# Reordering small products and first attention scores in a fused RWKV, tanh feed-forward and top-1 expert kernel

## The chip, the cores and the metric

The kernel runs on one core of a Trainium2 chip. The core has five engines that work side by side, each through its own instructions in a fixed order: TensorE (PE in the profile, with PEld for loading weights), VectorE (DVE), ScalarE (ACT), GpSimd (POOL) and SyncE (SP), which here issues transfers. The metric is the device time of one execution in microseconds (us); less is better.

## The reference

Three stages follow each other, in fp32:

```python
# 1. RWKV attention: B=4, H=8, S=768, D=48; state (D x D) for each batch and head
for t in range(S):
    cur = einsum(u * k_t, v_t)                    # outer product
    y[t] = r_t @ (state + cur)
    state = w[:, None] * state + outer(k_t, v_t)
x = y as (3072, 384)
# 2. feed-forward, w_in (384, 2048), w_out (2048, 384)
h = x @ w_in
x = (h - tanh(h)) @ w_out
# 3. top-1 mixture of 8 experts, w1 (8, 384, 1024), w2 (8, 1024, 384)
logits = normed(x) @ normed(expert_emb).T / tau   # argmax picks the expert, softmax its weight
out[mask_e] = gate[mask_e] * (relu(x[mask_e] @ w1[e]) @ w2[e])
```

## The kernel before, in words

**Tiles and blocks.** The 3072 tokens are 24 tiles of 128; tile n belongs to batch n % 4 and is that batch's chunk n // 4. Three tiles make a block of 384 columns, of which there are eight. The state of a batch is carried from chunk to chunk in `st`. Tiles 0 to 2 are block 0, tiles 3 to 5 block 1, tiles 6 to 8 the third block (j = 2).

**Attention of one tile.** The recurrence is written as products. Keys and queries are multiplied with tables of decays (`decay_k` on POOL or VectorE, `decay_r` on VectorE). `scores` (16 products into two PSUM banks `pa`) gives the scores of eight heads. `diagonal` writes a tile `am` for each half of the heads that holds the bonus term on its diagonal: eight small ScalarE copies for tiles 0 to 5, two POOL products from tile 6 on. `causal` (VectorE) copies the scores above it into `am`. `values` multiplies `am` and the old state into a bank `py`, `result` writes its high and low parts into the block's tile `xt`, `state` adds the tile's product to the state. For tiles 0 to 5 the keys are turned by TensorE into a bank (`turned`, `ps_k`) and copied out by ScalarE (`turned_rows`, `ktok`). From tile 6 on POOL makes `ktok` (`decayed`) and the bonus `rk` (`bonus`), which VectorE sums (`sums`). The five operations from the decay to `decayed` are a tile's head.

**Feed-forward.** Hidden block f (128 of 2048 columns) of a token block is nine products in `ffn1` (fp32 is split into a high and a low part, three products for each of three slices) into a bank `ph`; ScalarE and VectorE turn it into `ghi` and `glo`; `ffn2` adds nine products into three accumulator banks, three steps later (`LAG`, `PLAG`).

**Early steps.** The first 22 steps are hidden blocks 0 to 5 of block 0 and all 16 of block 1. Beside them the kernel converts the weights, which come as 64-bit floats in 16 pieces, into fp32 (three integer operations on VectorE, a copy `wq` on ScalarE, a subtraction on POOL, L267), and makes eight extra columns of w_out by which the expert logits fall out of `ffn2`. Such a `Logits` takes three steps: `turn` (six transpositions into two banks `pt`, two ScalarE copies into `wt`, a tag of two buffers), in the next step `product` (12 products into `pl`), in the one after it `back`. The turns are in steps 1, 2, 4, 7, 9, 12, 16 and 19. The attention of tiles 3, 4 and 5 begins in steps 1, 2 and 3 (`attention_stage`). Some steps have products of ones ahead of their hidden block (`fill`, `IDLE`), which compute nothing that is used.

**The last steps of block 0.** The loop over j follows: j = 0 does block 0's hidden blocks 6 to 15 (n = 0 to 9), then come blocks 2 to 7. The attention of block j + 1 runs beside block j as a generator of 18 pieces, six for a tile: head; scores and causal; two empty; values, state and result; empty. During j = 0 it is that of the third block; (n + 1) * 18 // 8 pieces have been drawn after step n. So tile 6's head and scores are drawn at n = 0, its values at n = 2, tile 7's head and scores at n = 3, its values at n = 4, tile 8's head at n = 5, its scores at n = 6 and its values at n = 7. Block 1's last accumulation is at n = 2, behind the pieces of that n. Its `finish` then copies three rows into tiles `xr` and stores them, finds the expert of each token, and computes the gates (with a POOL power and a ScalarE exponential, L673 and L678).

**What sets the order.** Up to `startup.close()` the order on each engine is that of the program. Behind it a planner orders each engine: among the instructions that its own simulated time makes ready it takes the one that stands first in the program. The buffers of a tag, PSUM banks included (eight, one tag), are given out again when the last user of the old tile is done. `rk` and `xr` share a tag of two buffers. `tc.issue_after(x)` puts the instructions in its block behind x on x's engine. `fence[6]` puts tile 6's head behind instructions of step 9.

Of the kernel before, what the change touches and what calls it, by code (L numbers as in the profile page):

```python
# [9 lines left out]
F32R = mybir.dt.float32r  # L10
# [3 lines left out]
AF = mybir.ActivationFunctionType  # L14
# [15 lines left out]
def rwkv__then__tanh_ffn__then__top1_moe_kernel(  # L30
# [14 lines left out]
    nc = tc.nc  # L45
# [6 lines left out]
    P = 128  # L52
    HP = H // 2
    NCH = S // P
    NK = DM // P
    TB = 3
    NB = NT // (TB * P)
    TOK = TB * P
# [16 lines left out]
    DACT = True  # L75
# [3 lines left out]
    NATT = 12  # L79
    NATT0 = 8  # L80
    ICOL = 6
# [130 lines left out]
    mark = {}  # L212
# [116 lines left out]
    class Att:  # L329
# [56 lines left out]

        def diagonal(self, on_act=False):
            self.am = []
            for g in range(2):
                a = work.tile([P, HP, P], F32, name="am", bufs=4)  # L390
                if on_act:
                    for q in range(HP):
                        nc.scalar.activation(out=a[:, q, :], in_=ident, func=AF.Copy, scale=self.cd[:, q, g:g + 1])
                else:
                    nc.gpsimd.tensor_tensor(out=a, in0=ident[:, None, :].to_broadcast([P, HP, P]),  # L395
                                            in1=self.cd[:, :, g:g + 1].to_broadcast([P, HP, P]), op=ALU.mult)
                self.am.append(a)
# [80 lines left out]

    def attn_tile(n, xt):
        t = Att(n, xt)  # L480
        with ExitStack() as es:
            for x in fence.pop(n, ()):
                es.enter_context(tc.issue_after(x))
            t.decay_r(nc.vector)
            t.decay_k(nc.gpsimd)
            t.bonus(nc.gpsimd)
            t.sums()
            t.diagonal()
            t.decayed()
        yield  # L490
        t.scores(range(HP))
        t.causal()
        yield
        yield
        yield

        t.values()
        t.state()
        t.result()
        yield  # L500
        yield

    xts = {}
    fence = {}
# [9 lines left out]
    def attention(j):  # L514
        xts[j] = work.tile([P, NK, 2, TOK], F32R, name="xt")
        for n in range(TB * j, TB * j + TB):
            if 2 * TB + 1 < n + 1 < NTILE:
                load_rkv(n + 1)
            yield from attn_tile(n, xts[j])

# [715 lines left out]
    def attention_stage(i):  # L1236

        later = []
        for n, first in zip(range(TB, 2 * TB), START):
# [6 lines left out]
            if i == first + 1:  # L1246
# [3 lines left out]
                t.turned()  # L1250
                t.diagonal(DACT)
                t.turned_rows()
            elif i == first + 2:
# [22 lines left out]
    def step2(j, i, g):  # L1276
        if i == spans[j][0]:
            accs[j] = [ps.tile([P, DL], F32, tag="p", name=f"acc{t}") for t in range(TB)]
        ffn2(i, spans[j], g, wout, accs[j])

    steps = [(0, f) for f in range(FA)] + [(1, f) for f in range(NF)]
    spans[0] = (0, FA)
# [3 lines left out]
    for i in range(len(steps) + 1):  # L1286
# [33 lines left out]
        for f in later:  # L1320
            f()
        if i in turns:
            c = turns[i]
            logits.append(Logits(c, ready[2 * c + 1][0]))
            logits[c].turn()
            done.add(2 * c + 1)
        if i - 2 in turns:
            logits[turns[i - 2]].back()
        if i - 1 in turns:
            logits[turns[i - 1]].product()  # L1330
        if m < NF:
# [3 lines left out]
        if i == 9:  # L1335
            fence[2 * TB] = mark["glo"], last[1]
        load_next()
# [4 lines left out]
        if i == ISTORE:  # L1342
            store_x(1, xts[1])
    del xts[1]

# [16 lines left out]
    for j in (0, *range(2, NB)):  # L1362
        xt = xts.pop(j)
        store_x(j, xt)
        att = attention(max(j + 1, 2)) if j + 1 < NB else iter(())
        na = 0
        natt = NATT if j > 0 else NATT0
        for n, i in enumerate(range(*spans[j])):
            ph = ffn1([win(p, i) for p in range(2)], columns_of(xt), NK, TOK)
            pend.append((j, i, small_tanh(ph, squares(ph), j * NF + i)))  # L1370
            while na < (n + 1) * 18 // natt:
                next(att, None)
                na += 1
# [103 lines left out]
```

## Time and profile before

| | |
|---|---|
| median of 3 runs | 812.74 us (811.16 to 815.42) |
| profiled execution | 813.03 us, of which the span from the first to the last instruction is 811.4 |
| mean granted TensorE clock | 0.980 of full speed |
| TensorE busy | 778.0 us (96% of the span) |
| VectorE, ScalarE, POOL busy | 506.7, 452.0 and 284.1 us |

Times in the profile count from the start of the span. A group of instructions is named by engine, source line and by the tiles that it writes and reads (`out<-in`). An entry in brackets gives the idle time of the engine just before the instruction and the instruction that ended it. The granted clock (PEclk) is 1.00 where TensorE had its 2.4 GHz for the whole stretch and 0.50 where it had 1.2 GHz. Ends of matmuls are modelled.

### The profile page before, as it was taken

The page shows a single profiled execution, that of the slowest core. Times are in us where ns is not written, and L with a number is a line of the kernel's source. Part 1 is how long each engine was busy: PE and PEld are TensorE (multiplying, and loading weights), DVE is VectorE, ACT ScalarE, POOL GpSimd, SP SyncE. Part 2 cuts the span into 40 slices and gives each one's busy share as a digit, 9 for nine tenths or more (in the row PEclk, how much of TensorE's full clock was granted, in tenths as well). Part 3 has the DMA queues.
Part 4 walks back from the last instruction along what each step waited for, and adds up shares of the span by engine and source line. Part 5 has one row for each costly group of instructions (what it writes and reads, how often), then busy time and mean ns, then how long its engine had stood idle before and what let it go on. Part 6 is the DMA issues. An engine that isn't in the chain of part 4 may idle for free. (4 is left out here: it accounts for less than half of the span.)

```text
span 811.4 us, 15572 instructions
## 1 busy us (share of the span) xinstructions
PE 778.0 (96%) x5938; PEld 729.3 (90%) x5938; DVE 506.7 (62%) x1080; ACT 452.0 (56%) x1044; POOL 284.1 (35%) x296
## 2 busy tenths in 40 slices
PE   8899999999999999999999999999899999999992
PEld 5679898889999999999999999999789999999992
DVE  7977974766765866875865865686544435554510
ACT  5676686547456556566566567684443444454421
POOL 3721640563550750750741610333340313331111
PEclk9899999999999999999999999999999999999997
DMA  8834350223330240331231210331733445554300
GB/s 275 284 89 134 111 194 1 85 83 122 106 114 23 67 155 21 83 125 43 86 116 54 86 45 15 120 96 31 229 102 118 137 129 166 175 171 143 111 28 30
DMA packets 41861, 87.33 MB, mean 108 GB/s; under 512 B 9744, under 2 KB 21440, under 8 KB 40754
## 3 DMA queue, kind: packets, MB, share of 16 engines
q1 hardware_dynamic: 37042, 76.74, 29.1%
q0 software_dynamic: 4320, 9.51, 3.6%
q8 instruction: 48, 0.79, 0.4%
q14 instruction: 35, 0.29, 0.2%
q10 hardware_dynamic: 416, 0.00, 0.0%
HBM read 67.46 MB, written 19.47 MB: 107 GB/s over the span
## 5 line engine op out<-in xcount | busy, mean ns | idle before, releaser
L534 PE MATMUL ph<-xt,wq 128*128 128x384 f32 (+2 forms) x1712 | 343.4, 343 | 2.2 <-ACT wt L284 1.4
L534 PEld LDWEIGHTS ph<-xt,wq 128*128 128x128 f32 x1712 | 304.2, 190 | 7.8 <-issue 1.7
L545 PE MATMUL acc<-wq,ghi 128*128 128x392 f32 (+2 forms) x1120 | 289.9, 344 | 0.9 <-ACT ghi L610 0.5
L545 PEld LDWEIGHTS acc<-wq,ghi 128*128 128x128 f32 (+1 forms) x1120 | 200.8, 187 | 6.5 <-issue 1.2
L545 PE MATMUL acc<-wq,glo 128*128 128x392 f32 (+2 forms) x560 | 185.6, 342 | 0.0
L581 ACT ACTIVATE z<-ph 128x384 f32<-128x384 f32 x128 | 62.6, 489 | 89.1 <-PE ph L534 88.6
L545 PEld LDWEIGHTS acc<-wq,glo 128*128 128x128 f32 (+1 forms) x560 | 104.3, 187 | 1.3 <-DVE glo L597 0.3
L592 ACT ACTIVATE ghi<-ph 128x384 fp32r<-128x384 f32 x128 | 62.7, 490 | 67.7 <-DVE ph L591 62.9
L590 DVE TENSOR_TENSOR ph<-ph,z 128x384 f32<-128x384 f32 x128 | 71.8, 561 | 45.2 <-ACT z L581 44.8
L597 DVE TENSOR_TENSOR glo<-ph,ghi 128x384 fp32r<-128x384 f32 x128 | 70.9, 554 | 40.9 <-ACT ghi L592 39.7
L764 POOL DMA_INDIRECT out_dram<-ob,gts x27 | 28.7, 1063 | 156.2 <-ACT ob L842 150.7
L582 ACT ACTIVATE q<-z,sb_t 128x384 f32<-128x384 f32 x128 | 78.9, 617 | 3.7
L591 DVE SCALAR_TENSOR_TENSOR ph<-q,ph 128x384 f32<-128x384 f32 x128 | 71.7, 560 | 12.0 <-ACT q L582 3.3
L611 DVE SCALAR_TENSOR_TENSOR glo<-ph,ghi 128x384 fp32r<-128x384 f32 (+2 forms) x56 | 31.4, 563 | 75.5 <-ACT ghi L610 59.8
L594 ACT ACTIVATE mk<-z,lz_t 128x384 bf16<-128x384 f32 x128 | 77.1, 602 | 0.0
L610 ACT ACTIVATE ghi<-ph 128x384 fp32r<-128x384 f32 (+2 forms) x56 | 27.7, 496 | 73.6 <-PE ph L534 72.5
L811 DVE TENSOR_TENSOR wq<-eraw,wq 128x768 fp32r<-128x768 f32 x60 | 58.2, 1008 | 16.0 <-ACT wq L810 11.9
L810 ACT ACTIVATE wq<-eraw 128x768 fp32r<-128x768 f32 x64 | 50.5, 838 | 10.4 <-DMA eraw<-in_moe_w_dram 10.3
L267 POOL TENSOR_TENSOR wq<-wraw,wq 128x768 fp32r<-128x768 f32 (+1 forms) x17 | 30.8, 1810 | 62.6 <-ACT wq L266 62.6
L380 POOL TENSOR_TENSOR rk<-rkv 128x384 f32<-128x384 f32 x18 | 18.4, 1020 | 90.2 <-DMA xs<-xr 42.4
L395 POOL TENSOR_TENSOR am<-ident,cd 128x512 f32<-128x512 f32 x36 | 37.3, 1059 | 11.2 <-DVE cd L385 10.5
L346 POOL TENSOR_TENSOR tt<-tt,tab_k 112x512 f32<-112x512 f32 x20 | 33.2, 1660 | 21.8 <-DMA tt<-in_cols_dram 20.6
(282 smaller groups left out, 886.8 us busy)
## 6 DMA issues: line engine op xcount, KB each, us to landing
eraw<-in_moe_w_dram SPq DMA_DIRECT2D x32, 768.0 KB, 4.9
rkv<-in_rows_dram SPq DMA_DIRECT2D x18, 640.0 KB
tt<-in_cols_dram SPq DMA_DIRECT2D x22, 448.0 KB, 4.0
xd<-xt SPq DMA_DIRECT2D x8, 1152.0 KB, 8.4
wraw<-in_moe_w_in_dram SPq DMA_DIRECT2D x8, 768.0 KB
wraw<-in_moe_w_out_dram SPq DMA_DIRECT2D x8, 768.0 KB, 7.1
xs<-xr SPq DMA_DIRECT2D x21, 192.0 KB, 2.1
rkv<-in_rows_dram SPq DMA_DIRECT2D x4, 256.0 KB, 10.4
```

The costliest lines, as they stand in the source:

```text
L395: nc.gpsimd.tensor_tensor(out=a, in0=ident[:, None, :].to_broadcast([P, HP, P]), in1=self.cd[:, :, g:g + 1].to_broadcast([P, HP, P]), op=A ...
L534: nc.tensor.matmul(out=ph, lhsT=lhs[a][:, kk, :], rhs=rhs(b, kk), start=(kk == 0 and p == 0), stop=(kk == nk - 1 and p == 2))
L545: mm = nc.tensor.matmul(out=acc[t], lhsT=g[a][:, t * P:t * P + m], rhs=rhs(b, i), start=(i == span[0] and p == 0), stop=(i == span[1] - 1 ...
L581: nc.scalar.activation(out=z, in_=ph, func=AF.Square)
L582: nc.scalar.activation(out=q, in_=z, func=AF.Square, scale=SS, bias=sb_t)
L590: nc.vector.tensor_tensor(out=ph, in0=ph, in1=z, op=ALU.mult)
L591: nc.vector.scalar_tensor_tensor(out=ph, in0=q, scalar=KC, in1=ph, op0=ALU.add, op1=ALU.mult)
L592: nc.scalar.activation(out=ghi, in_=ph, func=AF.Copy)
L594: nc.scalar.activation(out=mk, in_=z, func=AF.Relu, bias=lz_t, accum_out=zx[:, step:step + 1])
L597: mark["glo"] = nc.vector.tensor_tensor(out=glo, in0=ph, in1=ghi.bitcast(F32), op=ALU.subtract).ins
L810: nc.scalar.activation(out=hi[c][:, a], in_=t[:, a], func=AF.Copy)
L811: engs[s % len(engs)].tensor_tensor(out=lo[c][:, a], in0=t[:, a], in1=hi[c][:, a].bitcast(F32), op=ALU.subtract)
```

## The change

Four edits. In the early steps `back` and `product` of earlier pieces stand ahead of `turn` of the next one, which changes something in steps 2, 4 and 9. `diagonal` takes a function that it calls after its first four copies, ordered behind the fourth of them; in the early steps this is `turned_rows`, which stood behind all eight. The fence of tile 6's head now holds for tile 7's too. The generator of the third block's attention is made before the steps, and one piece is drawn at the end of each of the last four (tile 6's head in step 18, its scores in step 19, two empty ones); in the loop of block 0 the remaining fourteen are drawn so that 5 + 3n // 2 have been drawn after step n. Tile 6's values are then at n = 0, tile 7's head and scores at n = 2, its values at n = 4, tile 8's head and scores at n = 6, its values at n = 8. The tile `xt` of the block is asked for just before the first values instead of with the generator's start.

```diff
-    NATT0 = 8
...
-        def diagonal(self, on_act=False):
+        def diagonal(self, on_act=False, between=None):
...
                     for q in range(HP):
-                        nc.scalar.activation(out=a[:, q, :], in_=ident, func=AF.Copy, scale=self.cd[:, q, g:g + 1])
+                        ins = nc.scalar.activation(out=a[:, q, :], in_=ident, func=AF.Copy,
+                                                   scale=self.cd[:, q, g:g + 1]).ins
+                    if between and g == 0:
+                        with tc.issue_after(ins):
+                            between()
...
-    def attn_tile(n, xt):
-        t = Att(n, xt)
+    def attn_tile(n):
+        t = Att(n, None)
...
+        j = n // TB
+        if j not in xts:
+            xts[j] = work.tile([P, NK, 2, TOK], F32R, name="xt")
+        t.xt = xts[j]
         t.values()
...
     def attention(j):
-        xts[j] = work.tile([P, NK, 2, TOK], F32R, name="xt")
...
-            yield from attn_tile(n, xts[j])
+            yield from attn_tile(n)
...
-                t.diagonal(DACT)
-                t.turned_rows()
+                t.diagonal(DACT, t.turned_rows)
...
+    third = attention(2)
     steps = [(0, f) for f in range(FA)] + [(1, f) for f in range(NF)]
...
+        if i - 2 in turns:
+            logits[turns[i - 2]].back()
+        if i - 1 in turns:
+            logits[turns[i - 1]].product()
         if i in turns:
             c = turns[i]
             logits.append(Logits(c, ready[2 * c + 1][0]))
             logits[c].turn()
             done.add(2 * c + 1)
-        if i - 2 in turns:
-            logits[turns[i - 2]].back()
-        if i - 1 in turns:
-            logits[turns[i - 1]].product()
...
-            fence[2 * TB] = mark["glo"], last[1]
+            fence[2 * TB] = fence[2 * TB + 1] = mark["glo"], last[1]
...
+        if len(steps) - 4 <= i < len(steps):
+            next(third)
     del xts[1]
...
-        att = attention(max(j + 1, 2)) if j + 1 < NB else iter(())
-        na = 0
-        natt = NATT if j > 0 else NATT0
+        att = attention(j + 1) if 0 < j < NB - 1 else third
+        na = 0 if j > 0 else 4
...
-            while na < (n + 1) * 18 // natt:
+            while na < ((n + 1) * 18 // NATT if j > 0 else 5 + 3 * n // 2):
                 next(att, None)
```

## Rows read from the trace of the kernel before

**Rows 1.** Busy time by stretch: PE, PEld, DVE, ACT, POOL, then PEclk, DMA share, GB/s

```profile
...
45.00:49.00 4.00, 4.00 (x22) 3.04 (x23) 2.26 (x5) 2.10 (x5) 0.74 (x1) 0.57 0.64 197
...
164.00:168.00 4.00, 4.00 (x15) 3.73 (x14) 2.10 (x5) 1.97 (x5) 2.05 (x4) 0.58 0.09 3
180.00:520.00 340.00, 340.00 (x2931) 326.07 (x2926) 234.83 (x514) 210.67 (x517) 132.72 (x130) 1.00 0.24 79
69.00:106.00 37.00, 35.63 (x252) 32.62 (x251) 33.99 (x75) 25.02 (x59) 20.50 (x16) 1.00 0.37 121
...
120.00:140.00 20.00, 20.00 (x122) 17.52 (x120) 10.55 (x22) 12.37 (x31) 1.87 (x1) 1.00 0.04 17
...
```

**Rows 2.** Waits of TensorE from 60 to 180 us: total, times, longest

```profile
...
PE py L438 <- DVE am L412: 2.6, 1, 2.6
PE ph L534 <- ACT wt L284: 1.4, 1, 1.4
```

**Rows 3.** Timeline of TensorE, 42 to 58 us: start, duration, line, operation

```profile
...
42.51 0.90 PE L282 MATMUL pt<-ident,wraw 128*128 128x128 f32 x6
44.98 1.38 PE L291 MATMUL pl<-wt,ent 128*32 128x128 f32 x12 [1.57 <-ACT ktok L357]
46.28 1.46 PE L525 MATMUL ph<-ones 128*128 128x384 bf16 x4
47.29 2.46 PE L534 MATMUL ph<-xt,wq 128*128 128x384 f32 x9
...
53.50 0.85 PE L291 MATMUL pl<-wt,ent 128*32 128x128 f32 x12
...
54.96 0.81 PE L525 MATMUL ph<-ones 128*128 128x384 bf16 x4
55.47 1.86 PE L534 MATMUL ph<-xt,wq 128*128 128x384 f32 x9
...
```

**Rows 4.** Timeline of ScalarE, 39 to 45 us

```profile
...
39.61 0.49 ACT L581 ACTIVATE z<-ph 128x384 f32<-128x384 f32 x1 [3.69 <-PE ph L534]
...
42.11 2.44 ACT L393 ACTIVATE am<-ident,cd 128x128 f32<-128x128 f32 x8
44.45 0.47 ACT L357 ACTIVATE ktok<-ps_k 128x384 f32<-128x384 f32 x1
...
```

**Rows 5.** Timeline of VectorE, 35 to 46 us

```profile
...
35.39 1.57 DVE L343 TENSOR_TENSOR cols<-cols,tab_r 112x512 f32<-112x512 f32 x1
...
38.90 0.69 DVE L343 TENSOR_TENSOR tt<-tt,tab_r 112x512 f32<-112x512 f32 x1
...
44.56 0.73 DVE L412 COPY_PREDICATED am<-cmask,pa 128x512 f32<-128x512 uint8 x1
...
```

**Rows 6.** Timeline of POOL, 95 to 162 us

```profile
...
95.21 1.30 POOL L346 TENSOR_TENSOR tt<-tt,tab_k 112x512 f32<-112x512 f32 x1
...
97.44 2.01 POOL L376 TENSOR_TENSOR ktok<-rkv,ktab 128x384 f32<-128x384 f32 x2
...
104.22 1.87 POOL L267 TENSOR_TENSOR wq<-wraw,wq 128x768 fp32r<-128x768 f32 x1
...
155.42 1.02 POOL L380 TENSOR_TENSOR rk<-rkv 128x384 f32<-128x384 f32 x1
...
159.30 2.09 POOL L395 TENSOR_TENSOR am<-ident,cd 128x512 f32<-128x512 f32 x2
...
```

**Rows 7.** DMA issues of SP, 106 to 156 us

```profile
...
106.12 5.03 SPq L231 DMA_DIRECT2D wraw<-in_moe_w_out_dram  x2
...
151.13 4.56 SPq L633 DMA_DIRECT2D xs<-xr  x3
...
```

**Rows 8.** Timeline of ScalarE at 161 us

```profile
...
161.46 0.22 ACT L678 ACTIVATE ex<-l 128x24 f32<-128x24 f32 x1 [4.66 <-DVE l L676]
...
```

**Rows 9.** Timeline of VectorE and TensorE, 113 to 118 us

```profile
...
113.88 1.01 DVE L259 SCALAR_TENSOR_TENSOR wraw<-wraw,bits 128x512 int32<-128x512 int32 x2
...
116.87 0.87 PE L282 MATMUL pt<-ident,wraw 128*128 128x128 f32 x6
...
```

## The prediction

> **What bounds the kernel now.** I read the busy times by stretch first. From 180 to 520 us TensorE is busy for the whole 340 us [rows 1]: there nothing but fewer or faster products could help, and the change alters none. What the change can win lies before 180 us. So I next asked the waits view for TensorE between 60 and 180 us: it has two entries, 2.6 us for the causal copy of an attention tile and 1.4 us for a copy of transposed weights [rows 2]. Third, the timeline between 40 and 58 us: one hole of 1.57 us in front of the twelve logits' products at 44.98, ended by ScalarE's copy of the turned keys [rows 3]. Fourth, the granted clock behind these holes: over 45 to 49 us it is 0.57 and over 164 to 168 us 0.58 [rows 1], so each is followed by some 4 us in which TensorE spends most of the time at 1.2 instead of 2.4 GHz. Four microseconds at 0.57 lose 4 x 0.43 = 1.72 us, at 0.58 lose 1.68. The two holes with their slow tails are worth 1.57 + 1.72 = 3.3 us (early) and 2.6 + 1.68 = 4.3 us (late), 7.6 us together. The hole of 1.4 us has no slow tail that I count.
>
> **Part one, the early hole: products before transpositions, keys between the diagonals.** In step 2 the program now turns the second piece of w_out (six transpositions, 0.90 us at 42.51) and then multiplies the first piece (44.98) [rows 3]. The transpositions need two PSUM banks, the products a third. By the program eight banks are taken then: two scores of tile 4, the turned keys of tile 4, the step's hidden block, two banks of the conversion, two of the transpositions. The one that comes free is that of the turned keys: ScalarE copies them at 44.45 for 0.47 us, behind eight diagonal copies that begin at 42.11 and last 2.44 us [rows 4]. With the edit the copy stands behind four of the eight: 42.11 + 1.22 = 43.33, done at 43.80, which is 1.12 us earlier.
>
> With the new order the products run at 42.51 and, at the duration of the next such group (0.85 us at 53.50 [rows 3]), end at 43.36. The first three transpositions follow (0.45 us), the second three wait for the bank until 43.80 and end near 44.3. Then comes the hidden block of step 3, with four filling products ahead of it: a ninth bank, first given back by the first causal copy of tile 4, which VectorE runs at 44.56 for 0.73 us [rows 5]. Neither row has idle time ahead of it, so VectorE passes a saving on. A further edit, the fence on tile 7, takes tile 7's decay multiplication (0.69 us at 38.90 [rows 5]) out of this run, so that copy ends at 45.29 - 0.69 = 44.60. The filling products start at about 44.7 instead of 46.28 [rows 3]: 1.6 us. If the two holes that remain (0.05 and 0.35 us) leave the clock up, fills and hidden block take 55.47 + 1.86 - 54.96 = 2.37 us as in step 4 instead of 47.29 + 2.46 - 46.28 = 3.47 [rows 3]: 1.1 us more. Bounds: 3.3 us (all of the hole and its tail) and nothing (if the bank goes to something else, or the weights' copies come to end last). Below nothing I exclude: the second piece's products come 10 us later (53.50), so transpositions that are 0.85 us late hold nobody up. I take the middle between 1.6 and 2.7, **2.1 us**.
>
> For the keys of tile 3 the edit can cost: if the plan puts the copy between the diagonals although the transpositions on TensorE end later, ScalarE and its queue (diagonals of the other half, a weight split, two transposition copies) stand still for up to some 2 us. The cover is ScalarE's idle 3.69 us ahead of 39.61 [rows 4]; I cost it at nothing, and at 2 us if that cover were gone. In steps 4 and 9 only a single transposition passes six others; nothing.
>
> **Part two, tile 7's head.** The causal copy of tile 7 is late because its diagonal is: POOL, which works in order, runs the bonus of tile 7 at 155.42 and its diagonals at 159.30 for 2.09 us [rows 6]. Its keys were multiplied long before, together with tile 6's, at 97.44 [rows 6]; the inputs were there. What was not there is a buffer: the bonus tile shares a tag of two buffers with the three rows that block 1's finish stores, the program asks for those three first, and the stores are issued from 151.13 on over 4.56 us [rows 7]. The bonus starts when they have landed. In the new program tile 7's head is drawn at n = 2, ahead of that finish (it comes at the end of the same n), so its bonus gets a buffer before the rows do, and POOL can run it where it ran tile 6's. Removed from the way: all of the wait, 2.6 us, and its tail, 1.68 us: **4.3 us**.
>
> What moves with it. POOL gets, beside tile 6's work from 95 us on, tile 7's decay (1.3 us), two bonus products (2.0) and two diagonals (2.1): 5.4 us more, in front of or between weight subtractions as that at 104.22 [rows 6]. VectorE gets 0.69 us of decay and a short reduction where it is busy 33.99 of 37 us [rows 1]; TensorE has work there, and the hidden blocks are three steps ahead of their use: nothing, 0.7 us if it is not hidden. One decay multiplication beside a busy POOL took 1.57 us (35.39) instead of 0.69 [rows 5], so 0.9 us more at most by rows. The Trainium skill (SBUF — State Buffer, "Who interferes with whom") says that a VectorE instruction with two SBUF inputs and a reading GpSimd instruction exclude each other for the whole instruction. By that the price would be one whole POOL instruction, here up to 1.87 us, and the sum 6.4 - 1.9 = 4.5 us if all of it showed. By the row the sum would be 6.4 - 0.9 = 5.5 us; I count neither, for the same cover.
>
> **Part three, first scores in the last early steps.** Tile 6's sixteen score products go from n = 0 to step 19, its values from n = 2 to n = 0; scores of tile 7 from n = 3 to 2, tile 8's stay at 6, its values go from n = 7 to 8. Products only change places. Tile 8's two loads on SP are issued at n = 2, and their buffer comes free two steps sooner; they pass the finish's stores in SP's queue and hold nobody. In step 19 three accumulators, two hidden blocks, two transposition banks and two scores make nine banks: a short wait is possible, at most like the 1.4 us [rows 2]. I take nothing, since ScalarE (12.37 of 20 us) and VectorE (10.55) empty banks at once there [rows 1]. The deferred output tile is drawn when block 1's last hidden block has read its buffer: nothing.
>
> **The sum.** 4.3 + 2.1 = 6.4 us. The profiled execution took 813.03 us; 806.6 of it would be left. The median shown is 812.74, 0.29 below, so **806.3 us**. Half a percent, about what a measurement of this kernel can tell from no change, is 4.1 us: the bound is 808.7.
>
> **Rivals.** (A) The early part gives nothing since another bank ends last: 812.74 - 4.3 = 808.4. (B) The late hole stays in another form: ScalarE stood still 4.66 us for the exponential of block 1's finish until 161.46 [rows 8], and everything behind it, the squares of a hidden block too. Against it: the finish goes over POOL for its root, and POOL's work for tile 7 stands in front of that now [rows 6]; it goes away. If it still holds TensorE: 812.74 - 2.1 = 810.6. (C) Slower: POOL, in order, gets the whole of tile 7's head in front of the subtraction at 104.22. That is 5.4 us, 1.0 for its keys and some 2 us of waiting for VectorE's sums, 8.4 in all. The buffer for a further piece of w_out is free only then (SP waits at 106.12 and loads at once [rows 7]), its conversion ends at 113.88 + 1.01, its transpositions stand at 116.87 [rows 9]: 2.0 us of slack. TensorE would wait 6.4 and run slowly for 1.7: 8.1 against 6.4 won, so 814.4. It decides from a delay of 6.7 us on. Against it: the subtractions come earlier in the program, and POOL took them at once when they were ready. (D) The change doesn't do what it says: the order on each engine is made by a planner, which may take the same instructions in nearly the same order, or shift a wait into the later blocks: 812.7.
>
> **How the numbers follow.** Forecast 0.52 (own range 803.7 to 808.0), A 0.20, B 0.10, C 0.08, D 0.10. The range leaves out C and D, and reaches from 812.74 - 7.6 - 1.4 (both holes and the third one) = 803.7 to B and a little over, 811.0. Faster than 808.7: nearly all of the forecast and half of A, 0.61. Slower than 816.8: C where the delay is some 3 us longer than worked out, or D where a wait that is shifted into the later blocks brings a slow tail of its own, together 0.07. The rest, with B, the other half of A and most of C and D, 0.32.
>
> **What would show it.** Right: no TensorE wait for the causal copy near 160 us and a granted clock of 1.00 there; tile 7's bonus on POOL near 100 us; the keys' copy of tile 4 between its diagonals; the logits' products ahead of the six transpositions without a hole. Wrong: a hole of over 1 us between 40 and 60 us with a slow tail, waits for transposition copies near 117 or 130 us, or new holes after 180 us.

## The result and the profile after

The changed kernel takes 804.16 us (median of 4 runs, 802.11 to 807.7) against 811.95 for the kernel before beside it (810.04 to 815.42): ratio 0.9915, 95% interval 0.9886 to 0.9943. The prediction said 806.3 with a range from 803.7 to 811.0.

The profiled execution after took 807.7 us with a span of 806.1, the slowest of the four. Its first hidden block begins 4.5 us later than in the profile of before (25.71 against 21.17 us), although both programs have the same instructions in the same order until then. So the stretches below are compared from that block on, not from the start of the span.

The windows view of the kernel after, over the places of [rows 1]; with the later start the early one lies some 4.5 us further on, at 49 to 53 us. Columns: window, length, PE, PEld, DVE, ACT, POOL busy, PEclk, DMA share, GB/s.

```profile
49.00:53.00 4.00, 3.73 (x48) 3.14 (x48) 2.51 (x6) 3.25 (x8) 1.49 (x1) 1.00 0.44 113
164.00:168.00 4.00, 4.00 (x33) 3.63 (x32) 3.46 (x7) 2.87 (x8) 3.44 (x4) 1.00 0.67 44
180.00:184.00 4.00, 3.01 (x16) 2.43 (x15) 3.40 (x6) 2.63 (x8) 1.85 (x2) 1.00 0.33 135
```

The granted clock is 1.00 at both places where it was 0.57 and 0.58. TensorE's busy time drops to 3.01 of 4 us at 180 us: a new hole. The waits view of TensorE from 60 to 180 us, which had two entries in [rows 2], keeps a short one:

```profile
PE ph L540 <- ACT wt L283: 0.3, 1, 0.3
```

The place of [rows 3] on TensorE after the change:

```profile
46.89 0.85 PE L290 MATMUL pl<-wt,ent 128*32 128x128 f32 x12
47.67 0.62 PE L281 MATMUL pt<-ident,wraw 128*128 128x128 f32 x3
49.27 0.63 PE L281 MATMUL pt<-ident,wraw 128*128 128x128 f32 x3 [0.97 <-DVE am L415]
49.73 0.81 PE L531 MATMUL ph<-ones 128*128 128x384 bf16 x4
50.25 1.87 PE L540 MATMUL ph<-xt,wq 128*128 128x384 f32 x9
```

The products (L290) stand ahead of the transpositions (L281) as predicted, but the hole is still there: 0.97 us ahead of the second three transpositions, ended by VectorE's causal copy. ScalarE there, the place of [rows 4]:

```profile
46.53 2.45 ACT L392 ACTIVATE am<-ident,cd 128x128 f32<-128x128 f32 x8
48.89 0.47 ACT L356 ACTIVATE ktok<-ps_k 128x384 f32<-128x384 f32 x1
```

The keys' copy still stands behind all eight diagonal copies and ends at 49.36, later than the transpositions began. The bank came from the causal copy instead, on VectorE (the place of [rows 5]):

```profile
48.48 0.72 DVE L415 COPY_PREDICATED am<-cmask,pa 128x512 f32<-128x512 uint8 x1
```

POOL, where [rows 6] showed tile 7's bonus at 155.42:

```profile
98.07 1.01 POOL L379 TENSOR_TENSOR rk<-rkv 128x384 f32<-128x384 f32 x1
...
101.28 1.01 POOL L379 TENSOR_TENSOR rk<-rkv 128x384 f32<-128x384 f32 x1
...
104.21 1.89 POOL L266 TENSOR_TENSOR wq<-wraw,wq 128x768 fp32r<-128x768 f32 x1
...
110.91 2.04 POOL L398 TENSOR_TENSOR am<-ident,cd 128x512 f32<-128x512 f32 x2
112.91 1.87 POOL L266 TENSOR_TENSOR wq<-wraw,wq 128x768 fp32r<-128x768 f32 x1
120.91 1.89 POOL L266 TENSOR_TENSOR wq<-wraw,wq 128x768 fp32r<-128x768 f32 x1 [6.13 <-ACT wq L265]
...
157.43 1.01 POOL L379 TENSOR_TENSOR rk<-rkv 128x384 f32<-128x384 f32 x1 [6.68 <-ACT xr L637]
```

Two bonuses run near 100 us, and tile 7's diagonals at 110.91. POOL is idle for 6.13 us ahead of the subtraction at 120.91, so the 5.4 us of added work delayed no weights from there on, and TensorE waits for none. The wait for the row buffers now falls to the next tile: its bonus waits 6.68 us until 157.43, and nobody waits for that. The new hole on TensorE:

```profile
181.22 0.44 PE L540 MATMUL ph<-xt,wq 128*128 128x384 f32 x1
182.65 1.66 PE L540 MATMUL ph<-xt,wq 128*128 128x384 f32 x8 [0.99 <-DVE xt L449]
```

Block 2's first hidden block waits 0.99 us for the low part of tile 8, whose values moved from n = 7 to n = 8.

**Stretches.** ScalarE copies each hidden block once (`z`, 128 copies), so its k-th copy marks the same hidden block in every kernel. The start of the 15th, 46th and 128th copy, counted from the start of the first, is the ruler used below (us):

| kernel | 15th | 46th | 128th |
|---|---|---|---|
| before | 83.70 | 215.21 | 523.78 |
| after | 80.34 | 206.31 | 514.80 |
| keys between alone (same order as before) | 81.95 | 211.51 | 521.37 |
| products first alone | 80.94 | 211.95 | 521.89 |
| fence alone | 81.73 | 212.52 | 522.07 |
| these three | 80.32 | 212.40 | 523.00 |
| third block early alone | 82.42 | 209.19 | 519.38 |
| before, bonus in place | 83.71 | 214.57 | 523.24 |
| after without fence | 80.99 | 208.99 | 519.18 |
| after without keys between | 80.37 | 206.42 | 515.27 |
| after, tile 7's head late | 80.35 | 210.35 | 519.69 |
| after, tile 8's values sooner | 81.06 | 205.65 | 514.31 |
| after, keys forced | 79.88 | 205.98 | 515.60 |
| after, both of these | 80.27 | 204.86 | 513.76 |

Against the profile of before, after wins 3.36 us up to the 15th copy, 8.90 up to the 46th and 8.98 up to the 128th. The 4.53 us later start takes half of that away in this one pair of profiles (the end gives 0.85 back): 4.53 - 8.98 - 0.85 = -5.3, which is 806.1 - 811.4.

Each row is one execution, and the ruler itself scatters. Up to the 15th copy TensorE has the same order in four of these kernels (before, keys between, third block early, bonus in place); they show 83.70, 81.95, 82.42 and 83.71. It has the same order, too, in after, after without keys between and after with tile 8's values sooner, which show 80.34, 80.37 and 81.06. So a difference between two rows of the first column shows little when it is under 0.7 us, or under 1.8 us where one of the two may hold a stretch of slow clock.

### The profile page after: what moved, and what is told of

Read it like the earlier page. It is cut to its first block, busy times and chain, and to the rows that moved or that the text cites. A ratio compares the mean times of both kernels' runs of the same rounds, so it can differ in the third digit from the quotient of the medians.

```text
span 806.1 us, 15566 instructions
## 1 busy us (share of the span) xinstructions
PE 776.5 (96%) x5938; PEld 730.0 (91%) x5938; DVE 508.2 (63%) x1080; ACT 450.7 (56%) x1044; POOL 283.8 (35%) x296
## 5 line engine op out<-in xcount | busy, mean ns | idle before, releaser
L817 DVE TENSOR_TENSOR wq<-eraw,wq 128x768 fp32r<-128x768 f32 x60 | 55.3, 961 | 18.7 <-ACT wq L816 17.1
```

The costliest lines, as they stand in the source:

```text
L817: engs[s % len(engs)].tensor_tensor(out=lo[c][:, a], in0=t[:, a], in1=hi[c][:, a].bitcast(F32), op=ALU.subtract)
```

## The experiments

Ratios are to the kernel before, timed beside each kernel; its medians were 812.97, 813.17 and 813.53 us in the three groups of four.

**One part alone: products first.**

```diff
+        if i - 2 in turns:
+            logits[turns[i - 2]].back()
+        if i - 1 in turns:
+            logits[turns[i - 1]].product()
         if i in turns:
```

> The kernel before with one part of the change: back and product of earlier pieces ahead of the turn of the next one. My theory: the 1.57 us hole ahead of the logits' products near 45 us and its stretch at half clock go, since the twelve products need no bank that the six transpositions hold; without the fence of tile 7 the causal copy stays where it was, so 0.7 us of the 2.2 us that the whole change wins there is missing: 1.4 to 2.2 us less from the first hidden block to the first back, and 809.8 to 810.6 us in all from 811.95; the wait for the causal copy of tile 7 near 159 us (2.6 us) stays. Rival 1: the early gain comes from the fence and not from the order, then 0 to 0.5 us here and a hole of over 1 us ahead of the fills. Rival 2: the early stretch varies by itself by as much, then the profile shows no connection between the order and the stretch's length.

Measured: 812.12 us, ratio 0.9988 (0.9969 to 1.0007). The 809.8 to 810.6 us of my theory did not come; rival 1's hole of over 1 us did. Its TensorE near 44 us and near 85 us:

```profile
42.30 0.85 PE L291 MATMUL pl<-wt,ent 128*32 128x128 f32 x12
43.08 0.62 PE L282 MATMUL pt<-ident,wraw 128*128 128x128 f32 x3
44.94 0.63 PE L282 MATMUL pt<-ident,wraw 128*128 128x128 f32 x3 [1.24 <-ACT ktok L357]
...
85.46 1.84 PE L534 MATMUL ph<-xt,wq 128*128 128x384 f32 x9 [0.29 <-ACT wt L284]
```

The hole has only changed its place, from the products to the transpositions: hidden block 3 starts 25.00 us after block 0 (46.11 - 21.11), exactly as with the old order (46.16 - 21.16 in the next experiment). The stretch to the 15th copy is 1.01 us shorter than in that experiment all the same: the wait for transposed weights near 88 us, 1.4 us in [rows 2], is 0.29 here, and it is 0.3 in every kernel that has this edit and 1.4 in every one that has not. ScalarE shows why:

```profile
84.94 0.47 ACT L284 ACTIVATE wt<-pt 128x384 f32<-128x384 f32 x1
85.31 0.89 ACT L266 ACTIVATE wq<-wraw 128x768 fp32r<-128x768 f32 x1
```

The copy of the transposed weights goes ahead of a weight conversion of 0.89 us. In the kernel before the conversion goes first (87.05, then the copies at 87.83). So the edit wins where I had costed it at nothing, and not where I had aimed it.

**One part alone: keys between the diagonals.**

```diff
-                t.diagonal(DACT)
-                t.turned_rows()
+                t.diagonal(DACT, t.turned_rows)
```

> The kernel before with one part of the change: the copy of the turned keys is called after the first four of the eight diagonal copies. My theory after the comparison of the two traces: the planner keeps ScalarE's order as it was (the copy stood behind all eight after the change too), so the time is that of before, ratio 1.000 within 0.002, and what this run shows is how much executions of one and the same order differ. Rival, the step of my prediction: the copy of tile 4's keys moves 1.1 us forward and the hole at 43 to 45 us shrinks by as much, 1.1 us plus part of the slow clock, some 810 us.

Measured: 813.68 us, ratio 1.0008 (0.9982 to 1.0035). The order of instructions is that of before on every engine, so this is a second look at before, and it shows something that the first hid. TensorE near 45 us, then the windows:

```profile
44.86 0.85 PE L291 MATMUL pl<-wt,ent 128*32 128x128 f32 x12 [1.56 <-ACT ktok L357]
```

```profile
45.00:49.00 4.00, 4.00 (x58) 3.16 (x54) 2.83 (x6) 3.00 (x7) 1.01 (x1) 1.00 0.68 197
164.00:168.00 4.00, 4.00 (x59) 3.30 (x58) 3.22 (x7) 2.29 (x7) 3.31 (x5) 1.00 0.33 27
```

The hole of 1.56 us is there, but the clock behind it is 1.00, and it is 1.00 at 164 us too, behind a wait of 1.70 us for the causal copy of tile 7 where the profile of before has 2.65. So the same order can run with or without the slow stretches of [rows 1]. The execution that had them is 1.75 us longer up to the 15th copy (83.70 - 81.95) and 3.70 up to the 46th, and 0.95 of the rest is its longer wait.

How often the slow stretch comes, the other profiles with these holes tell. Behind the early hole the kernel with the bonus in place has it (1.57 us of hole; all of it 4.5 us later), the third block early alone and the fence alone do not (2.36 and 1.42 us of hole, clock 1.00 from 44 to 54 us). Behind the late hole products first alone (a wait of 1.93 us) and the fence alone (1.67 us) have it. Windows of these three, bonus in place first:

```profile
49.00:53.00 4.00, 3.36 (x19) 2.39 (x20) 2.94 (x6) 2.76 (x7) 0.00 (x0) 0.59 0.69 196
160.00:164.00 4.00, 3.92 (x16) 3.72 (x17) 1.61 (x5) 0.78 (x2) 3.20 (x4) 0.57 0.08 2
160.00:164.00 4.00, 3.30 (x13) 3.07 (x14) 2.23 (x6) 0.94 (x3) 3.37 (x4) 0.62 0.07 1
```

The early slow stretch is thus in two of five profiles, the late one in three of four.

**One part alone: the fence of tile 7.**

```diff
-            fence[2 * TB] = mark["glo"], last[1]
+            fence[2 * TB] = fence[2 * TB + 1] = mark["glo"], last[1]
```

> The kernel before with one part of the change: the fence that holds tile 6's head back holds tile 7's too. My theory: VectorE loses a decay multiplication of 0.69 us near 39 us, the causal copy of tile 4 comes 0.7 us sooner, but the products stand behind the transpositions still and these wait for the copy of the keys by ScalarE, so the hole of 1.57 us in front of the products stays and only what comes after it shrinks: 0 to 0.5 us, 811.5 to 812. The wait near 159 us stays: 2.6 us. Rival: the fence makes the whole early gain, 2.1 us, 809.8. Second rival: the fence alone moves tile 7's bonus or diagonal on POOL and so changes the late wait, by up to 4 us in either direction.

Measured: 812.21 us, ratio 0.9991 (0.9973 to 1.0008); 0.22 us to the 15th copy. The hole ahead of the products is 1.42 us, ended by the causal copy now and not by the keys' copy as my theory had it. The hole stays, as the theory expected, and 0.22 us lies within the scatter of the ruler. The wait near 159 us is 1.67 us, not 2.6.

**One part alone: the third block early.**

```diff
+        if len(steps) - 4 <= i < len(steps):
+            next(third)
...
-            while na < (n + 1) * 18 // natt:
+            while na < ((n + 1) * 18 // NATT if j > 0 else 5 + 3 * n // 2):
```

> The kernel before with one part of the change: the first four pieces of the third block's attention in the last four early steps and the other fourteen by the new formula. My theory: tile 7's head is asked for ahead of block 1's finish, its bonus gets a buffer near 100 us instead of 155, the wait of 2.6 us for the causal copy near 159 us and its 1.7 us of slow clock go, and a wait of about 1 us for tile 8's low part may come near 182 us: 3.5 to 5 us less, 807 to 808.5 us; the early hole of 1.57 us near 43 us stays. Rival: the late wait comes from POOL's queue or from the finish and not from the order of the requests for the buffer, then it stays at over 2 us or appears at another product, 811 to 812 us. Second rival: without the fence tile 7's head goes far ahead in POOL's order and delays a weight subtraction, a new wait of several us near 60 to 120 us, 814.

Measured: 809.43 us, ratio 0.9966 (0.9945 to 0.9986), a gain of some 2.8 us, less than the 3.5 to 5 of my theory. TensorE's waits from 30 to 230 us:

```profile
PE pl L290 <- ACT ktok L356: 2.4, 1, 2.4
PE ph L536 <- ACT wt L283: 1.4, 1, 1.4
...
PE ph L536 <- DVE xt L445: 1.0, 1, 1.0
```

The wait for the causal copy of tile 7 is gone, and the new wait of 1.0 us for the low part of tile 8 belongs to this part. The early hole is 0.8 us longer than before; ScalarE's diagonals begin 0.42 us later than in the execution above (42.41 against 41.99), after 0.65 us of waiting for a weight conversion on VectorE. The drawing did not do that: each engine has the order of before up to 97 us. It is one execution against another.

**The buffer alone.** Nothing is drawn sooner; the bonus is written over its input.

```diff
-            self.rk = work.tile([P, H, D], F32, name="rk", tag="xr")
+            self.rk = self.r
```

> The kernel before with one line changed: from tile 6 on the bonus product is written over its input instead of into a buffer of the tag that it shares with the rows of block 1's finish. Nothing is drawn sooner in the program. My theory: the buffer is all that held tile 7's bonus; POOL runs it near 100 us as after the change, the 2.6 us wait near 159 us and its slow clock go: 3.5 to 4.5 us less than before, 807.5 to 808.5 us. Rival 1: it is the place in the program that counts (the head and scores of tile 7 are drawn at n = 3), POOL still runs the bonus near 155 us, 812. Rival 2: the wait goes but TensorE waits for ScalarE's exponential of block 1's finish instead, 810 to 812.

Measured: 812.74 us, ratio 0.9993 (0.9964 to 1.0023). The theory's mechanism came out and its gain did not. POOL runs four diagonals (tiles 6 and 7) at 106.92, and the wait near 160 us is gone. But TensorE then stands still for longer, one tile on, and its clock is 0.65 from 180 to 184 us. POOL, DVE and PE of this kernel:

```profile
106.92 4.08 POOL L395 TENSOR_TENSOR am<-ident,cd 128x512 f32<-128x512 f32 x4
...
175.24 1.00 POOL L380 TENSOR_TENSOR rkv<-rkv 128x384 f32<-128x384 f32 x1 [3.59 <-DMA rkv<-in_rows_dram]
```

```profile
178.17 0.55 DVE L385 TENSOR_REDUCE cd<-rkv 128x8 f32<-128x384 f32 x1 [3.23 <-POOL rkv L381]
...
179.10 1.33 DVE L412 COPY_PREDICATED am<-cmask,pa 128x512 f32<-128x512 uint8 x2
```

```profile
179.88 0.64 PE L438 MATMUL py<-am,rkv 128*32 128x128 f32 x4 [4.10 <-DVE am L412]
```

Read from below: tile 8's values wait 4.10 us for its causal copy; that stands in VectorE's order behind the sums of tile 9's bonus; those wait for POOL, and POOL for tile 9's rows. SP issued their load at 168.08, behind a gate store of block 1's finish at 167.64, and they landed 7 us later. Freeing one tile's head moved the wait on to the next tile, behind a load that comes late.

**After without the fence.**

```diff
-            fence[2 * TB] = fence[2 * TB + 1] = mark["glo"], last[1]
+            fence[2 * TB] = mark["glo"], last[1]
```

> The kernel after without the fence of tile 7. My theory: tile 7's decay multiplication goes back into VectorE's run near 39 us, the causal copy of tile 4 ends 0.7 us later and with it the second three transpositions, the wait for it grows from 1.0 to about 1.7 us and may bring a stretch of slow clock: 0.7 to 1.8 us slower than after, 804.9 to 806. Rival 1: the fence is worth nothing, 804.2. Rival 2: without it tile 7's head on POOL goes ahead of weight work and costs several us, 808 or more.

Measured: 808.54 us, ratio 0.9931 (0.9909 to 0.9952). The second three transpositions wait 1.32 us, for the keys' copy, which ends 49.72; the causal copy ends 50.37, too late to help. The 15th copy comes 0.65 us later than after, just under the theory's 0.7 to 1.8. The median is further off than the 804.9 to 806 that I expected, and lies where rival 2 had it (808 or more). But rival 2's mechanism is not in the profile: tile 7's decay runs on POOL at 42.81 for 1.31 us, and POOL then stands 2.97 us until ScalarE hands it the next weights. Up to the 46th copy this profile loses 2.68 us; part of it lies behind the hole near 182 us, where the clock is 0.69 from 184 to 188 us in this execution, the slowest of the six. What the rest of the median is made of stays open.

**After with tile 8's values sooner.**

```diff
-            while na < ((n + 1) * 18 // NATT if j > 0 else 5 + 3 * n // 2):
+            while na < ((n + 1) * 18 // NATT if j > 0 else 4 + (n + 1) * 14 // 8):
```

> The kernel after with another rate of drawing beside block 0: 4 + (n + 1) * 14 // 8 pieces instead of 5 + 3n // 2, so that tile 8's values come at n = 7 again instead of n = 8. My theory: the 1.0 us wait of block 2's first product for the low part of tile 8 near 182 us goes, since the values stand one step (some 7 us) sooner; the wait near 159 us stays away: 0.5 to 1.3 us less than after, 802.9 to 803.7. Rival 1: that wait is hidden in another one at the transition (weights' loads, the high part), 804.2. Rival 2: tile 7's values come sooner too and wait for the diagonal again, 2 us or more slower.

The new rate does more than that: it draws tile 7's head at n = 1 and its values at n = 3, and tile 8's head and scores at n = 5, one step sooner each.

Measured: 804.58 us, ratio 0.9902 (0.9868 to 0.9935). The median missed my 802.9 to 803.7, and the ratio cannot be told from that of after. The wait near 182 us is gone: from 170 to 230 us TensorE has no wait left. From the 15th to the 46th copy it takes 124.59 us against 125.97 after, but its 15th copy came 0.72 us later.

**After with the keys' copy forced between.**

```diff
-                        ins = nc.scalar.activation(...)
+                        with tc.issue_after(self.kins) if g == 1 and self.n == TB + 1 and between else ExitStack():
+                            ins = nc.scalar.activation(...)
...
-                            between()
+                            self.kins = between()
```

> The kernel after with the last four diagonal copies of tile 4 put behind the copy of its turned keys, so that the keys' copy does stand between the diagonals, as the change meant. My theory: the bank of the keys comes 1.2 us sooner, the second three transpositions need not wait for the causal copy, and the wait of 1.0 us near 49 us goes, but the fills and the hidden block behind it need the bank that the causal copy gives back and wait for it then: 0 to 0.5 us of gain, 803.7 to 804.2. Rival: all of the 1.0 us is won, 803.2. Second rival: the diagonal's second half comes 0.5 us later and so the values of tile 4, a wait of 0.5 us elsewhere, 804.7.

Measured: 805.85 us, ratio 0.9905 (0.9887 to 0.9924). ScalarE and TensorE:

```profile
42.07 1.28 ACT L393 ACTIVATE am<-ident,cd 128x128 f32<-128x128 f32 x4
43.26 0.47 ACT L356 ACTIVATE ktok<-ps_k 128x384 f32<-128x384 f32 x1
```

```profile
43.22 1.19 PE L281 MATMUL pt<-ident,wraw 128*128 128x128 f32 x6
44.75 0.81 PE L532 MATMUL ph<-ones 128*128 128x384 bf16 x4 [0.34 <-DVE am L416]
```

This is what the prediction drew: copy behind four diagonals, six transpositions in one go, fills at 44.75. The fills' bank is the next limit, with a wait of 0.34 us. What it is worth is not shown: 0.46 us to the 15th copy (80.34 - 79.88) is inside my 0 to 0.5 but also inside the scatter of the ruler, the 128th copy is 0.80 us later than after, and the median missed my 803.7 to 804.2.

**After without the keys' edit.**

```diff
-                t.diagonal(DACT, t.turned_rows)
+                t.diagonal(DACT)
+                t.turned_rows()
```

> The kernel after with the keys' edit undone: the copy of the turned keys is called behind all eight diagonal copies again. My theory: the planner gave ScalarE the same order with and without this edit, so the time is that of after, 804.2 us within 1.5, ratio to before 0.9915 as there; it also gives after's time a second time, on the chip of this call. Rival, the step of my prediction: without the edit the copy of tile 4's keys comes 1.1 us later, the time is 1 to 2 us longer, 805 to 806, and the wait near 49 us is over 1.5 us.

Measured: 805.67 us, ratio 0.9909 (0.9876 to 0.9942); the copies of the table agree with after within 0.5 us. The median alone lies in the rival's 805 to 806 too. What decides is the trace: ScalarE, VectorE, POOL and SP have their instructions in the same order as after, the keys' copy stands behind all eight diagonal copies in both, and the wait near 49 us is 1.18 us, under the rival's 1.5. That edit does nothing here, and the change's ratio is found a second time.

**The three early edits together** (the diffs of the first three, on before).

> The kernel before with the three early edits (products first, keys between, fence of tile 7) and without the third block's early pieces. My theory after the single edits: up to step 14 the order wins 1.0 us, nearly all of it at the hole of 1.4 us near 88 us and not at the one near 44 us, and the fence 0.65 us: 1.7 us less there than an execution of before whose clock stayed up, 3.4 us less than the profiled one; the wait for the causal copy of tile 7 near 158 us stays at 1.5 to 2.6 us; ratio to before 0.997 to 0.999. Rival, my prediction's sum: 2.1 us or more, all of it before the first back, ratio 0.9974 or lower. Second rival: the early part frees engines for tile 7's head too and the late wait goes as well, ratio 0.992.

Measured: 810.70 us, ratio 0.9966 (0.9946 to 0.9985). To the 15th copy it gains 1.63 us on the execution of the same order as before (81.95 - 80.32), as worked out. The ratio is a little lower than my 0.997 to 0.999 and lies in the range of the first rival, my prediction's sum, so the time does not decide between them. My figure for the late wait missed: TensorE waits 2.95 us near 152 us, but for block 1's finish and not for the causal copy. Its VectorE, POOL and TensorE:

```profile
150.42 2.03 DVE L644 TENSOR_TENSOR l<-l,mx 128x24 f32<-128x24 f32 x1
152.48 0.92 DVE L646 SCALAR_TENSOR_TENSOR ix<-l,iom 128x24 f32<-128x24 f32 x1
...
153.65 0.82 DVE L650 TENSOR_TENSOR oh<-iom,mx 128x24 bf16<-128x24 f32 x1
```

```profile
149.65 1.80 POOL L346 TENSOR_TENSOR tt<-tt,tab_k 112x512 f32<-112x512 f32 x1 [2.02 <-DMA tt<-in_cols_dram]
151.42 0.99 POOL L376 TENSOR_TENSOR ktok<-rkv,ktab 128x384 f32<-128x384 f32 x1
```

```profile
154.53 0.19 PE L653 MATMUL pk<-oh,tri 128*128 128x8 bf16 x1 [2.95 <-DVE oh L650]
```

**After with tile 7's head late again.** One number of the drawing; tile 7's head and scores come at n = 3.

```diff
-            while na < ((n + 1) * 18 // NATT if j > 0 else 5 + 3 * n // 2):
+            while na < ((n + 1) * 18 // NATT if j > 0 else 5 + 3 * n // 2 - 2 * (n == 2)):
```

> The kernel after with one number of the drawing changed: tile 7's head and scores are drawn at n = 3, as in the kernel before, and not at n = 2; all other pieces where the change has them. My theory: block 1's finish asks for its three row buffers ahead of tile 7's bonus again, POOL runs the bonus near 155 us instead of 100, and the wait of TensorE for the causal copy of tile 7 near 158 us returns with 1.5 to 3 us, in some executions with slow clock behind it: 2 to 4.5 us slower than after, 806 to 808.5. Rival: what won was the drawing of tile 6's head and scores in the early steps, then nothing returns, 804. Second rival: tile 7 is wanted late enough now, the wait moves but is under 0.5 us, 804.2 to 804.7.

Measured: 811.26 us, ratio 0.9980 (0.9955 to 1.0004). POOL and TensorE of this kernel:

```profile
152.62 1.02 POOL L379 TENSOR_TENSOR rk<-rkv 128x384 f32<-128x384 f32 x1 [4.63 <-ACT xr L637]
...
156.49 2.07 POOL L398 TENSOR_TENSOR am<-ident,cd 128x512 f32<-128x512 f32 x2
```

```profile
160.77 0.41 PE L441 MATMUL py<-am,rkv 128*32 128x128 f32 x4 [2.17 <-DVE am L415]
```

With the request behind the finish's again, the bonus waits for the row buffer, runs at 152.62, and TensorE waits 2.17 us with a clock of 0.70 from 160 to 164 us. This takes 4.4 us up to the 128th copy (519.69 - 515.27) and 5.6 us of the medians (811.26 - 805.67), more than the 2 to 4.5 of my theory. The early drawing of tile 6, which stayed, makes little of the late gain by itself.

**After with both improvements** (tile 8's values sooner, keys forced).

> The kernel after with both improvements together: tile 8's values at n = 7 again, and tile 4's last four diagonal copies behind the copy of its keys. My theory: the 1.0 us wait near 182 us goes as it did alone, and 0.5 us of the wait near 49 us: 1.3 to 1.6 us less than after, 802.6 to 803, ratio to before 0.9895 to 0.9905. Rival: the one at 182 us had the slack to be hidden, then only 0.5 us, 803.7. Second rival: run to run differences of the start hide both, 804.

Measured: 803.32 us, ratio 0.9875 (0.9847 to 0.9902), 2.35 us less than the change without its keys' edit in the same group. No wait is left near 49 and near 182 us. Its interval overlaps with those of after, after without keys between, and after with each improvement alone, so that both improvements together are the fastest is likely and not shown; that each of these five beats before is shown.

## Why the prediction was right, and where it was not

**The late part was right in mechanism and about right in size.** Tile 7's bonus waited for a buffer that the finish's rows had asked for first. Drawing its head sooner puts the bonus near 100 us, the wait of 2.6 us is gone and the clock stays at 1.00 [rows 1, 2, 6]. I had 4.3 us. Undoing that one draw costs 4.4 us by the copies and 5.6 by the medians; the third block's part alone wins 2.8 by its ratio. Both have intervals of some 2 us to either side, and 4.3 lies between them. It was sized from one execution, though: its wait of 2.65 us is the longest of four with the late order of before (1.93, 1.70 and 1.67 in the others), and its slow stretch is missing in one of them. From the 15th to the 46th copy, after wins 3.6 us on an execution of the old order whose clock stayed up (129.56 - 125.97) and 5.5 on the profiled one. The gain is net of the new wait of 0.99 us at tile 8, which I had costed at nothing (values from n = 7 to n = 8): that term was mis-sized by about 1 us, 1.4 between the 15th and the 46th copy by the experiment that takes it back, which moves tile 7 and tile 8's head as well.

**The early part had the right sum from wrong terms.** I predicted 2.1 us up to the first back; the two profiles show 32.13 - 29.96 = 2.17. But 1.70 of it (32.13 - 30.43) is the slow clock that the profiled execution of before had behind its hole and another execution of the same order did not have. Over the four executions with the early order of before the 15th copy comes at 82.95 us on average, over the three with that of after at 80.59: 2.4 us apart, with pairs from 0.9 to 3.4. So 2.1 is a fair figure for the average, but I did not derive it as one. The step that failed: "With the edit the copy stands behind four of the eight". The planner left it behind all eight; undoing the edit in after changes nothing. So the products used 0.85 us of the hole, the transpositions inherited the rest, and the fills start 0.46 us sooner (24.48 - 24.02, counted from the first hidden block), not 1.6. The fence did more than I gave it: it takes away a decay that took 1.08 us beside POOL, the causal copy begins 0.97 us sooner (22.77 against 23.74 us after the first hidden block, with and without the fence, where I had 0.69), and with the products first it releases the bank that the keys' copy held too long.

**What I costed at nothing** was the order's gain at the 1.4 us hole near 88 us: 1.0 us. I had written that in steps 4 and 9 only a single transposition passes six others. That is true of the program, but the planner made more of it: ScalarE's copy of the transposed weights now passes a weight conversion of 0.89 us.

**The rivals.** (A) is nearest to the third block's part alone: 809.43 against 808.4. (B) did not come: ScalarE still waits 4.28 us for the exponential, until 162.54, and TensorE has no wait there. With the three early edits alone TensorE did wait 2.95 us for that finish, but for its VectorE instructions and not for the exponential. (C) did not come: POOL took the subtractions between tile 7's pieces. (D) held for one edit of the four. By the copies the parts add up nearly: on the execution with the clock up, 1.6 us early and 3.6 us late. The sum of the terms, 6.4 us, was right to 1.4 us of the 7.8 between the medians, and the early one came right partly by luck.

**Left open:** why the clock falls behind a hole in some executions and not in others, at the start as well, where that alone puts the first hidden block at 21.1 to 21.4 us in ten profiles, 22.6 in one and 25.7 to 25.9 in three; what the fence is worth, beyond the 0.65 us to the 15th copy; and how the 7.8 us between the medians divide exactly, since each experiment's interval is some 2 us to either side.

## What to carry to other kernels

A hole's slow tail in one profile is not a fixed term of the sum: here it was 1.7 of the 2.2 us by which the two early stretches differ, and with the same order it came in two of four profiles. Look at several executions and count it by the share that show it. Where buffers of one tag go to two users, the order of the requests in the program decides who waits, and taking back the move of one request past the other cost 5.6 of the 7.8 us by the medians; a buffer freed at one tile can uncover the load or the in-order queue of the next. After an edit of the program's order, read on the engine whether the planner followed it: one of four edits here changed no instruction's place.

## What the runs showed of the hardware

**The clock at the start.** Over the first 20 us the same instructions ran at different clocks. The windows view of before, then of after:

```profile
0.00:20.00 20.00, 17.13 (x194) 11.38 (x198) 15.50 (x45) 11.53 (x34) 6.01 (x42) 1.00 0.88 274
```

```profile
0.00:20.00 20.00, 17.37 (x117) 11.93 (x118) 12.07 (x38) 8.13 (x23) 6.02 (x42) 0.74 0.88 282
```

At 0.74 TensorE got through 117 matmuls where it did 194 at 1.00, and the first hidden block came 4.5 us later. In after nearly the whole loss lies in one stretch at 1.2 GHz:

```profile
8.00:18.00 10.00, 10.00 (x58) 7.74 (x57) 7.77 (x17) 6.18 (x21) 0.00 (x0) 0.50 1.05 360
```

Just before it TensorE had stood still for 1.33 us, until 7.19. In before it stood still for 1.41 us, until 7.10, and the clock stayed at 1.00. The kernel with the bonus in place and the one without the fence show the same 0.74 as after and start at 25.9. In the one with tile 7's head late it is 0.91 (0.50 from 8 to 10 us, 0.65 from 10 to 12) and the start is at 22.6. The other ten profiles show 1.00 and a start at 21.1 to 21.4.

**VectorE beside POOL.** In the kernel with the three early edits a 128x24 subtraction on VectorE took 2.03 us, where the median of its eight executions is 0.18. It starts at 150.42 and ends at 152.45: POOL's decay ends at 151.45 and its next product, begun at 151.42, at 152.41. So the short instruction sat through the rest of one POOL instruction and the whole of the next. The two short ones behind it, at 152.48 and 153.65, took 0.92 and 0.82 us where their medians are 0.18 and 0.17, and TensorE waited 2.95 us for the result of the last. The same in after, on VectorE and POOL:

```profile
166.66 2.47 DVE L342 TENSOR_TENSOR tt<-tt,tab_r 112x512 f32<-112x512 f32 x1
```

```profile
166.50 0.84 POOL L475 TENSOR_TENSOR st<-st,pw 112x384 f32<-112x384 f32 x1
167.29 1.28 POOL L345 TENSOR_TENSOR tt<-tt,tab_k 112x512 f32<-112x512 f32 x1
```

In [rows 5] such a decay takes 0.69 us; here it ends 0.56 us after POOL's second instruction. The Trainium skill (SBUF — State Buffer, "Who interferes with whom") says that a VectorE instruction with two SBUF inputs contends with a reading GpSimd instruction for a shared port under an exclusive lock. These rows agree, and the price here is 1.85 and 1.78 us, more than was left of the POOL instruction that ran when the VectorE instruction began (1.03 and 0.68 us). The prediction weighed this rule and counted nothing; in after nobody waited for it, in the kernel with the early edits TensorE did.
